# One PSUM bank for the seven first products of a pair, taken in four rounds between the second products

## The chip, the cores and the metric

The kernel runs on one core of one Trainium2 chip. The metric is the device time of one launch in microseconds, the median of several runs. The granted TensorE clock of the profiled execution is 1.000 of full speed.

## The reference

Linear attention in 8 batches of 8 heads, 576 positions of 64 values each, a root-mean-square norm over each head's output, and then a gated feed-forward layer over the 8 x 576 = 4608 rows of 512 values:

```python
kv = np.einsum('bhsd,bhse->bhde', k, v)
out = np.einsum('bhsd,bhde->bhse', q, kv)
rms = np.sqrt(np.mean(out * out, axis=-1, keepdims=True) + 1e-06)
attn = out / rms * g_norm                       # (8, 8, 576, 64)
x = attn.transpose(0, 2, 1, 3).reshape(4608, 512)
h = x @ w_in                                    # 512 -> 2048
g = h * (1.0 / (1.0 + np.exp(-h)))
return g @ w_out                                # 2048 -> 512
```

## The kernel before, in words

The 4608 rows are worked in 9 tiles of 512 (`t` = 0 to 8). The hidden width of 2048 is 16 blocks of 128 (`NF`). Each float32 operand is held as two rounded parts, an upper and a lower, and a product is three matmuls (upper by lower, lower by upper, upper by upper). A matmul here has 256 moving columns.

Tiles 0 and 1 take one block per step. From `t` = 2 on (the third tile) `pair_step` takes two blocks at once, block `i` and block `i + 8`, so a tile is 8 pairs and there are 56 pairs. A pair's two 128 x 512 results come from **seven products** instead of eight, by a scheme of the Strassen kind: sums of weight blocks (`make_sums`, kept in DRAM, loaded back for each pair by `load_sums` into the places `sums0` and `sums1`) meet sums of pieces of x (`sums_of_x`, split into parts by `make_operand`). `product(m, i, out)` issues the six matmuls of product `m` (L662). They are called P1 to P7 in this document, after `m`.

In before, a pair takes two PSUM banks of 512 columns, `bank` (halves `u`, `v`) and `other` (`y`, `z`), and issues all 42 matmuls in the order P1 to u, P2 to v, P6 to y, P7 to z, then P4 to u, P5 to v, P3 to y. ScalarE copies P1 to SBUF (`p1`, L713). VectorE forms the left half of `c1` (L714), `u2` (L715) and `u3` (L716), then `c2` (L726), and the right half of `c1` in two adds (L730, L731). `c1` and `c2` are the pair's two results; `upper_part` runs two Silu on ScalarE for each (L671 to `gh`, L672 in place), and `lower_part` subtracts on VectorE (L675, `gl`).

The **second product** multiplies `gh`, `gl` by blocks of `w_out` and accumulates in four other banks (`acc`, one for 128 rows). `project` is one item by one bank: six matmuls (L493). A pair hands two items to the next pair, so each pair runs eight such groups, 48 matmuls, of the pair before it. `due(n)` issues n groups. In before they stand in one stretch behind the seven products: `due(3)`, `due(3)` and the rest. At a tile's last pair the banks are copied out (L538, `ob`, in turns on VectorE and ScalarE) in the next tile's first pair and stored (L539).

The rest of the attention is spread between these as jobs, by step: `begin` runs the jobs that stand first in a step (copies of `kvm`, L281, and links of the norm's chain), `mid_jobs` and `last_jobs` the others: 80 small kv matmuls (L273) and the query products (L306 to L308) on TensorE, their copies (L312, L313) on ScalarE, the split of q (L293 on ScalarE, L294 on GpSimd), transposes, sums and scaling (L318, L319, L326, L334) on VectorE. `prepare` makes, in a tile's last pair, the next tile's operands: a cast on ScalarE (L653) and a subtraction on VectorE (L654) for each of seven, four after P7 and three after P3. Each engine works through its own queue in the order of the code, and the engines meet by semaphores.

Of the kernel before, what the change touches and what calls it, by code (L numbers as in the profile page):

```python
# [35 lines left out]
def linear_attention_rms_silu_ffn(  # L36
# [22 lines left out]
    nc = tc.nc  # L59
    B, NP, P, S = q.shape  # L60
# [3 lines left out]
    TN = 512  # L64
# [11 lines left out]
    gp = ctx.enter_context(tc.tile_pool(name="gp", bufs=LAG + 1))  # L76
# [28 lines left out]
    for i in range(4):  # L105
        nc.gpsimd.tensor_copy(
            out=both[32 * i:32 * i + 32, 32 * (i ^ 1):32 * (i ^ 1) + 32], in_=ident[32 * i:32 * i + 32, 32 * i:32 * i + 32]
# [106 lines left out]
    def run(*lists):  # L214

        for i in range(max(map(len, lists), default=0)):
            for calls in lists:
                if i < len(calls):
                    calls[i]()
# [255 lines left out]
    def h_bank():  # L475
        return ps_h.tile([P, 512], F32, name="hp", tag="h")
# [51 lines left out]
    def project(t, f, gh, gl, bank, n, cs):  # L528
        first, last = order(t)[0], order(t)[-1]
        w = parts["wo", f]  # L530
        ns = slice(n * P, (n + 1) * P)
        bank = bank[:, :cs.stop - cs.start]
        terms = ((gh, 1), (gh, 0), (gl, 0)) if t else ((gh, 0), (gl, 0), (gh, 1))
        for i, (g, a) in enumerate(terms):
            halves(bank, g[:, ns], w[:, a, cs], f == first and i == 0, f == last and i == 2)
        if f == last:
            ob = tmp.tile([P, S], F32, name="ob", tag="tmp")[:, :cs.stop - cs.start]
            (nc.scalar.copy if n % 2 else nc.vector.tensor_copy)(out=ob, in_=bank)  # L538
            nc.sync.dma_start(out=out[t * TN + n * P:t * TN + (n + 1) * P, cs], in_=ob)  # L539
# [4 lines left out]
    HF, H = NF // 2, TN // 2  # L544
    low, high = slice(0, H), slice(H, TN)
    sums_in_dram = dram.tile([HF, 2, P, 2, 2 * H], F32, name="sums_in_dram")
    operands, x_sums, once = {}, {}, {}
# [43 lines left out]
    def place(name, n, dtype):  # L591

        if name not in once:
            once[name] = block("wi", HF + 2 * n + 1, dtype).rearrange("p a (j n) -> p a j n", n=H)
        return once[name]

    def load_sums(i, *halves):

        for half in halves:
            to = place(f"sums{half}", half, F32R)  # L600
            nc.sync.dma_start(
                out=to.rearrange("p a j n -> p (a j n)").bitcast(F32),
                in_=sums_in_dram[i % HF, half].rearrange("p a n -> p (a n)"),
            )
# [18 lines left out]
    def operand(j):  # L623

        if j < 4:
            return x_second[:, j].rearrange("p a (k n) -> p a k n", k=2)
        if j not in operands:
            operands[j] = spare(j - 4, [P, 2, 2, H], F32R, f"operand{j}")
        return operands[j]
# [20 lines left out]
    def make_operand(m):  # L650
        j, x, _ = seven[m]
        upper, lower = operand(j)[:, 0], operand(j)[:, 1]
        nc.scalar.copy(out=upper, in_=x())  # L653
        nc.vector.tensor_tensor(out=lower, in0=x(), in1=upper.bitcast(F32), op=ALU.subtract)  # L654

    def product(m, i, out):
        j, _, a_of = seven[m]
        x = operand(j)
        n = 0
        for c in range(2):  # L660
            for a, b in ((0, 1), (1, 0), (0, 0)):
                nc.tensor.matmul(  # L662
                    out=out, lhsT=a_of(i, a, c), rhs=x[:, b, c], start=(n == 0), stop=(n == 5)
                )
                n += 1

# [2 lines left out]
    def upper_part(x, gh):  # L669

        nc.scalar.activation(out=gh, in_=x, func=AF.Silu)  # L671
        nc.scalar.activation(out=x, in_=x, func=AF.Silu)  # L672

    def lower_part(x, gh, gl):
        nc.vector.tensor_tensor(out=gl, in0=x, in1=gh.bitcast(F32), op=ALU.subtract)  # L675

    def pair_step(t, i, groups):


        g = t * NF + 2 * i  # L680
        fresh, later = i == HF - 1 and t + 1 < NT, i + 1 < HF or t + 1 < NT

        def due(n):
            while n > 0 and groups:
                n -= (groups[0][-1].stop - groups[0][-1].start) / DM
                project(*groups.pop(0))

        def begin(g):
            run(first_jobs.pop(g, ()))
            run(*[call() for call in chains.pop(g, ())])  # L690

        def prepare(*ms):

            for m in ms if fresh else ():
                make_operand(m)

        begin(g)
        bank, other = h_bank(), h_bank()
        u, v = bank[:, :H], bank[:, H:]
        y, z = other[:, :H], other[:, H:]  # L700
        if "gated" not in once:
            once["gated"] = gp.tile([P, TN], F32, name="gf", bufs=1)
        scratch = place("scratch", 3, F32)
        c1, c2 = [scratch[:, 0].rearrange("p j n -> p (j n)"), once["gated"]][::1 - 2 * (i % 2)]
        p1, u2 = scratch[:, 1, 0], scratch[:, 1, 1]
        u3 = p1
        if g == 2 * NF:
            due(4)
        product(1, i, u)
        product(2, i, v)  # L710
        product(6, i, y)
        product(7, i, z)
        nc.scalar.copy(out=p1, in_=u)  # L713
        nc.vector.tensor_tensor(out=c1[:, low], in0=v, in1=p1, op=ALU.add)  # L714
        nc.vector.tensor_tensor(out=u2, in0=y, in1=p1, op=ALU.add)  # L715
        nc.vector.tensor_tensor(out=u3, in0=z, in1=u2, op=ALU.add)  # L716
        if late_part:
            lower_part(*late_part.pop())
        if later:
            load_sums(i + 1, 0)  # L720
        prepare(1, 2, 6, 7)
        run(mid_jobs.pop(g, ()))
        product(4, i, u)
        product(5, i, v)
        product(3, i, y)
        nc.vector.tensor_tensor(  # L726
            out=c2.rearrange("p (a n) -> p a n", a=2), in0=bank.rearrange("p (a n) -> p a n", a=2),
            in1=u3.unsqueeze(1).to_broadcast([P, 2, H]), op=ALU.add
        )
        nc.vector.tensor_tensor(out=c1[:, high], in0=v, in1=u2, op=ALU.add)  # L730
        nc.vector.tensor_tensor(out=c1[:, high], in0=y, in1=c1[:, high], op=ALU.add)  # L731
        if later:
            load_sums(i + 1, 1)
        prepare(4, 5, 3)
        run(last_jobs.pop(g, ()))
        begin(g + 1)
        hi = [gp.tile([P, TN], F32R, name="gh") for _ in range(2)]
        lo = [gp.tile([P, TN], F32R, name="gl") for _ in range(2)]
        upper_part(c2, hi[0])
        lower_part(c2, hi[0], lo[0])  # L740
        due(3)
        run(mid_jobs.pop(g + 1, ()))
        upper_part(c1, hi[1])
        late_part.append((c1, hi[1], lo[1]))
        due(3)
        run(last_jobs.pop(g + 1, ()))
        due(len(groups))
        return [(t, i + HF, hi[0], lo[0]), (t, i, hi[1], lo[1])]


    first_jobs, mid_jobs, last_jobs, chains = {}, {}, {}, {}
# [86 lines left out]
    with tc.manual_schedule():  # L838
# [5 lines left out]
        for item in ORDER.split():  # L844
            kind, n = item.rstrip("0123456789"), int(item.lstrip("wiopbgq") or 0)
# [20 lines left out]
        p0, p1, p2, p3 = first  # L866
# [134 lines left out]
        for t in range(NT):  # L1001
# [3 lines left out]
            if t >= 2:  # L1005
                for i in range(HF):
                    pend = [(item, sums) for item in pair_step(t, i, [(*item, *old) for item, olds in pend for old in olds])]
                continue
            for step, f in enumerate(order(t)):
                g = t * NF + step  # L1010
# [80 lines left out]
```

## Time and profile before

| | |
|---|---|
| device time, three runs | 817.19, 817.23, 817.42 us; median 817.23 |
| span of the profiled execution | 815.8 us (its device time apart from the span is not recorded) |
| matmul instructions | 7484 |
| DVE instructions, busy | 1036, 533.9 us |
| ACT instructions, busy | 753, 361.6 us |
| POOL instructions, busy | 141, 145.7 us |
| DMA | 122.82 MB, mean 151 GB/s |

The profile is of one execution. PE is TensorE's matmuls and PEld its weight loads, DVE is VectorE, ACT ScalarE, POOL GpSimd and SP the engine that issues the DMAs. Matmuls overlap in the pipeline, so the time between two starts, not the duration of one, tells the rate. A row of the timeline has its start in the span, its time, the engine, the line, the operation, what it writes and reads, its shape and count, and in brackets the idle time before it with what ended that.

### The profile page before, as it was taken

To read this page: it belongs to the slowest core of one execution; us is meant where nothing else is said; L and a number is where in the kernel's file an instruction comes from. 1 tells how busy PE (TensorE), PEld (TensorE's weight loads), DVE (VectorE), ACT (ScalarE), POOL (GpSimd) and SP (SyncE) were. 2 spreads that over 40 slices of the span, in tenths; PEclk is the share of its full clock that TensorE was granted. 3 is DMA by queue.
4 is the path that set the end of the run, shared out by engine and by line. 5 is a ranking of instruction groups with operands and counts; after the bars stand their busy time and mean duration, and the time that the engine had idled before them with its cause. 6 is when DMAs were issued, how large, how long until landed. Compare 5 with 4: busy or idle time off the path is not lost.

```text
span 815.8 us, 18127 instructions
## 1 busy us (share of the span) xinstructions
PE 806.5 (99%) x7484; PEld 801.5 (98%) x7484; DVE 533.9 (65%) x1036; ACT 361.6 (44%) x753; POOL 145.7 (18%) x141
## 2 busy tenths in 40 slices
PE   7999999999999999999999999999999999999998
PEld 7899999999999999999999999999999999999998
DVE  4999956787566677656875767656865663464332
ACT  4887555434552355325532444245532432243222
POOL 2799783322110011000200020001100000000000
DMA  9994012356524444263436451445433343334321
GB/s 345 412 409 126 1 60 90 124 195 228 184 82 162 162 162 156 82 221 118 170 104 211 142 182 64 166 159 174 135 104 104 104 155 105 104 104 155 104 105 53
DMA packets 42277, 122.82 MB, mean 151 GB/s; under 512 B 4690, under 2 KB 4946, under 8 KB 42194
## 3 DMA queue, kind: packets, MB, share of 16 engines
q1 hardware_dynamic: 42194, 121.65, 42.4%
q8 instruction: 59, 0.97, 0.5%
q14 instruction: 24, 0.20, 0.1%
HBM read 103.81 MB, written 17.83 MB: 149 GB/s over the span
## 4 chain that ended last, share of the span: by engine, by line
PE 93%; DMA 4%; POOL 2%; issue 1%; SPq 1%; ACT 0%; POOLq 0%
PE acc L493 46%; PE hp L662 33%; PE hp L493 9%; DMA wo<-in_moe_w_out 3%; PE at L273 2%; PE at L306 1%; PE at L307 1%; PE at L308 1%; DMA early_wo<-in_q 1%; PE at L493 1%; POOL wo L212 1%; SPq L262 1%; POOL wi L212 0%; POOL gl L514 0%; POOL wo_full L178 0%
## 5 line engine op out<-in xcount | busy, mean ns | idle before, releaser
L493 PE MATMUL acc<-wo,gh 128*128 128x256 f32 x2272 | 354.6, 276 | 0.3 <-POOL wo L212 0.3
L493 PEld LDWEIGHTS acc<-wo,gh 128*128 128x128 f32 x2272 | 302.5, 188 | 0.7 <-POOL wo L212 0.5
L493 PE MATMUL acc<-wo,gl 128*128 128x256 f32 x1136 | 222.5, 276 | 0.0
L493 PEld LDWEIGHTS acc<-wo,gl 128*128 128x128 f32 x1136 | 171.7, 188 | 0.0
L662 PE MATMUL hp<-x_second,wi 128*128 128x256 f32 x1344 | 163.1, 276 | 0.0
L662 PEld LDWEIGHTS hp<-x_second,wi 128*128 128x128 f32 x1344 | 157.2, 188 | 0.0
L662 PE MATMUL hp<-operand,wi 128*128 128x256 f32 x1008 | 123.3, 276 | 0.0
L662 PEld LDWEIGHTS hp<-operand,wi 128*128 128x128 f32 x1008 | 118.4, 188 | 0.0
L294 POOL TENSOR_TENSOR ql<-q,qh 128x576 fp32r<-128x576 f32 x24 | 34.8, 1450 | 368.6 <-ACT qh L293 322.8
L713 ACT COPY wi<-hp 128x256 f32<-128x256 f32 x56 | 20.8, 372 | 136.5 <-PE hp L662 136.5
L671 ACT ACTIVATE gh<-gf 128x512 fp32r<-128x512 f32 x56 | 35.4, 632 | 91.9 <-DVE gf L726 80.4
L671 ACT ACTIVATE gh<-wi 128x512 fp32r<-128x512 f32 x56 | 35.5, 634 | 77.4 <-DVE wi L726 65.0
L714 DVE TENSOR_TENSOR gf<-hp,wi 128x256 f32<-128x256 f32 x28 | 11.9, 424 | 81.5 <-ACT wi L713 81.5
L714 DVE TENSOR_TENSOR wi<-hp,wi 128x256 f32<-128x256 f32 x28 | 11.9, 424 | 79.7 <-ACT wi L713 79.7
L493 PE MATMUL hp<-x_second,wi 128*128 128x256 f32 x384 | 46.3, 276 | 0.0
L675 DVE TENSOR_TENSOR gl<-wi,gh 128x512 fp32r<-128x512 f32 x56 | 38.4, 686 | 11.1 <-ACT wi L672 11.1
L493 PE MATMUL hp<-x,wi 128*128 128x256 f32 x360 | 44.5, 278 | 0.8 <-POOL x L444 0.8
L493 PEld LDWEIGHTS hp<-x_second,wi 128*128 128x128 f32 x384 | 44.9, 188 | 0.1
L675 DVE TENSOR_TENSOR gl<-gf,gh 128x512 fp32r<-128x512 f32 x56 | 39.3, 701 | 7.3 <-ACT gf L672 7.3
L493 PEld LDWEIGHTS hp<-x,wi 128*128 128x128 f32 x360 | 42.4, 188 | 1.2 <-POOL x L444 1.0
L715 DVE TENSOR_TENSOR wi<-hp,wi 128x256 f32<-128x256 f32 x56 | 23.8, 426 | 29.6 <-PE hp L662 29.6
L334 DVE SCALAR_TENSOR_TENSOR x<-o,gcol,yT 128x128 f32<-128x128 f32 (+7 forms) x52 | 41.2, 792 | 1.9
(143 smaller groups left out, 995.7 us busy)
## 6 DMA issues: line engine op xcount, KB each, us to landing
wi<-sums_in_dram SPq DMA_DIRECT2D x112, 512.0 KB, 3.4
out<-ob SPq DMA_DIRECT2D x35, 256.0 KB, 2.3
wi<-in_moe_w_in SPq DMA_DIRECT2D x16, 512.0 KB, 7.9
wo<-in_moe_w_out SPq DMA_DIRECT2D x16, 512.0 KB, 8.9
sums_in_dram<-sum_parts SPq DMA_DIRECT2D x16, 512.0 KB, 2.6
k<-in_k SPq DMA_DIRECT2D x28, 288.0 KB, 5.1
v<-in_v SPq DMA_DIRECT2D x28, 288.0 KB, 5.1
q<-in_q SPq DMA_DIRECT2D x28, 288.0 KB, 4.0
```

What stands on the lines that cost most here:

```text
L212: nc.gpsimd.tensor_tensor(out=w[:, 1, :], in0=full, in1=w[:, 0, :].bitcast(F32), op=ALU.subtract)
L262: nc.sync.dma_start(out=t, in_={"k": k, "v": v, "q": q}[name][self.b, self.c])
L273: nc.tensor.matmul(out=self.kv[h], lhsT=self.k[rows, c, :], rhs=self.v[rows, c, :], start=(start and r == 0), stop=(stop and r == 4),)
L294: (nc.vector if self.b == 1 else nc.gpsimd).tensor_tensor(out=self.ql, in0=self.q, in1=self.qh.bitcast(F32), op=ALU.subtract)
L334: nc.vector.scalar_tensor_tensor(out=to, in0=self.o[:, a:e], scalar=gcol, in1=self.yT, op0=ALU.mult, op1=ALU.mult)
L493: nc.tensor.matmul(out=to[:, at:at + 256], lhsT=stationary, rhs=moving[:, at:at + 256], start=start and at == 0, stop=stop and at == n - 256,)
L662: nc.tensor.matmul(out=out, lhsT=a_of(i, a, c), rhs=x[:, b, c], start=(n == 0), stop=(n == 5))
L671: nc.scalar.activation(out=gh, in_=x, func=AF.Silu)
L675: nc.vector.tensor_tensor(out=gl, in0=x, in1=gh.bitcast(F32), op=ALU.subtract)
L713: nc.scalar.copy(out=p1, in_=u)
L714: nc.vector.tensor_tensor(out=c1[:, low], in0=v, in1=p1, op=ALU.add)
L715: nc.vector.tensor_tensor(out=u2, in0=y, in1=p1, op=ALU.add)
```

## The change

The pair uses one bank, the same for all pairs (`once["products"]`), and its seven products come in four rounds, with two groups of second products behind each: P1 to u and P6 to v; P2 added on u and P7 on v; P4 to u anew and P5 to v; P3 added on v. Three products (P2, P7, P3) accumulate on what stands in PSUM. The copy of u and the adds change with that: ScalarE now also copies P1 + P2 to the left half of `c1` (L720), VectorE forms `u2` (L713), `u3` (L721), `c2` (L729) and the right half of `c1` (L740, one add). Jobs of the odd step now begin before P3. The lines of after are one or more higher than those of before from `product` on: the Silu are L672 and L673, the `gl` subtraction L676, and the line of the first products stays L662.

```diff
-    def product(m, i, out):
+    def product(m, i, out, fresh):
...
-                    out=out, lhsT=a_of(i, a, c), rhs=x[:, b, c], start=(n == 0), stop=(n == 5)
+                    out=out, lhsT=a_of(i, a, c), rhs=x[:, b, c], start=fresh and n == 0, stop=n == 5,
+                    skip_group_check=True,
...
-        bank, other = h_bank(), h_bank()
+        if "products" not in once:
+            once["products"] = h_bank()
+            once["gated"] = gp.tile([P, TN], F32, name="gf", bufs=1)
+        bank = once["products"]
         u, v = bank[:, :H], bank[:, H:]
-        y, z = other[:, :H], other[:, H:]
...
         if g == 2 * NF:
             due(4)
-        product(1, i, u)
-        product(2, i, v)
-        product(6, i, y)
-        product(7, i, z)
+        product(1, i, u, True)
+        product(6, i, v, False)
         nc.scalar.copy(out=p1, in_=u)
-        nc.vector.tensor_tensor(out=c1[:, low], in0=v, in1=p1, op=ALU.add)
-        nc.vector.tensor_tensor(out=u2, in0=y, in1=p1, op=ALU.add)
-        nc.vector.tensor_tensor(out=u3, in0=z, in1=u2, op=ALU.add)
+        nc.vector.tensor_tensor(out=u2, in0=v, in1=p1, op=ALU.add)
         if late_part:
             lower_part(*late_part.pop())
+        due(2)
+        run(mid_jobs.pop(g, ()))
+        product(2, i, u, False)
+        product(7, i, v, False)
+        nc.scalar.copy(out=c1[:, low], in_=u)
+        nc.vector.tensor_tensor(out=u3, in0=v, in1=p1, op=ALU.add)
         if later:
             load_sums(i + 1, 0)
         prepare(1, 2, 6, 7)
-        run(mid_jobs.pop(g, ()))
-        product(4, i, u)
-        product(5, i, v)
-        product(3, i, y)
+        due(2)
+        run(last_jobs.pop(g, ()))
+        product(4, i, u, True)
+        product(5, i, v, False)
         nc.vector.tensor_tensor(
             out=c2.rearrange("p (a n) -> p a n", a=2), in0=bank.rearrange("p (a n) -> p a n", a=2),
             in1=u3.unsqueeze(1).to_broadcast([P, 2, H]), op=ALU.add
         )
+        hi = [gp.tile([P, TN], F32R, name="gh") for _ in range(2)]
+        lo = [gp.tile([P, TN], F32R, name="gl") for _ in range(2)]
+        upper_part(c2, hi[0])
+        begin(g + 1)
+        due(2)
+        run(mid_jobs.pop(g + 1, ()))
+        product(3, i, v, False)
         nc.vector.tensor_tensor(out=c1[:, high], in0=v, in1=u2, op=ALU.add)
-        nc.vector.tensor_tensor(out=c1[:, high], in0=y, in1=c1[:, high], op=ALU.add)
+        lower_part(c2, hi[0], lo[0])
         if later:
             load_sums(i + 1, 1)
         prepare(4, 5, 3)
-        run(last_jobs.pop(g, ()))
-        begin(g + 1)
...
-        upper_part(c2, hi[0])
-        lower_part(c2, hi[0], lo[0])
-        due(3)
-        run(mid_jobs.pop(g + 1, ()))
         upper_part(c1, hi[1])
         late_part.append((c1, hi[1], lo[1]))
-        due(3)
         run(last_jobs.pop(g + 1, ()))
         due(len(groups))
```

On TensorE, a plain pair of `t` = 2 (the one of block 6) in before; `operand_2947`, `operand_2951`, `operand_2986` and the first `x_second` are the moving operands of P1, P2, P6 and P7, `wi_1341` carries P4, and the twelve of `wi_2945` are P5 and P3:

```order
L662 MATMUL hp<-operand_2947,wi_664 128x256 x6
L662 MATMUL hp<-operand_2951,wi_664 128x256 x6
L662 MATMUL hp<-operand_2986,wi_2943 128x256 x6
L662 MATMUL hp<-x_second,wi_2943 128x256 x6
L662 MATMUL hp<-x_second,wi_1341 128x256 x6
L662 MATMUL hp<-x_second,wi_2945 128x256 x12
L493 MATMUL acc<-wo_1583,gh 128x256 x4
```

The same pair on TensorE in the change, from the second products behind P1 and P6 to those behind P4 and P5, with the semaphores that each matmul waits for:

```order
L493 MATMUL acc<-wo_1583,gh 128x256 x4
L493 MATMUL acc<-wo_1583,gl 128x256 x2
L662 MATMUL hp<-operand_2951,wi_664 128x256 [waits DVE_49]
L662 MATMUL hp<-operand_2951,wi_664 128x256 x5
L662 MATMUL hp<-x_second,wi_2943 128x256 x6
L493 MATMUL acc<-wo_1583,gh 128x256 x4
L493 MATMUL acc<-wo_1583,gl 128x256 x2
L493 MATMUL acc<-wo_1583,gh 128x256 x4
L493 MATMUL acc<-wo_1583,gl 128x256 x2
L662 MATMUL hp<-x_second,wi_1341 128x256 [waits DVE_49]
L662 MATMUL hp<-x_second,wi_1341 128x256 x5
```

The 42 matmuls that stood together now stand in four pieces with 12 second products behind each, and the first matmul of P2 and of P4 waits for VectorE.

On ScalarE, the join of `t` = 3 and `t` = 4 in before, from the last three casts of `prepare` to the copy of P1 in the next tile's first pair (L713):

```order
L653 CAST x_second<-t_5172 128x512
L653 CAST x_second<-t_5170 128x512
L653 CAST x_second<-x_1_2123 128x512
L281 COPY kvm_90<-at 64x64 x2
L281 COPY kvm_91<-at 64x64 x2
L281 COPY kvm_92<-at 64x64 x2
L281 COPY kvm_93<-at 64x64 x2
L671 ACTIVATE gh<-wi_3138 128x512
L672 ACTIVATE wi_3138<-wi_3138 128x512
L671 ACTIVATE gh<-gf 128x512
L672 ACTIVATE gf<-gf 128x512
L713 COPY wi_3138<-hp 128x256
```

The same place on ScalarE in the change, from the Silu of `c2` to the copy of P1 (now L712):

```order
L672 ACTIVATE gh<-wi_3137 128x512
L673 ACTIVATE wi_3137<-wi_3137 128x512
L281 COPY kvm_90<-at 64x64 x2
L281 COPY kvm_91<-at 64x64 x2
L281 COPY kvm_92<-at 64x64 x2
L281 COPY kvm_93<-at 64x64 x2
L653 CAST x_second<-t_5150 128x512
L653 CAST x_second<-t_5148 128x512
L653 CAST x_second<-x_1_2123 128x512
L672 ACTIVATE gh<-gf 128x512
L673 ACTIVATE gf<-gf 128x512
L712 COPY wi_3137<-hp 128x256
```

The Silu of `c2` moved ahead of the kvm copies and the three casts; the Silu of `c1` and the copy of P1 stand behind them as before.

On TensorE, the first pair of `t` = 2 in the change, from its last second products to the next pair's first (`operand_2947` with `wi_457`):

```order
L493 MATMUL acc<-wo_1162,gh 128x256 x4
L493 MATMUL acc<-wo_1162,gl 128x256 x2
L662 MATMUL hp<-x_second,wi_965 128x256 x6
L662 MATMUL hp<-x_second,wi_2945 128x256 x12
L662 MATMUL hp<-operand_2947,wi_457 128x256 x6
L662 MATMUL hp<-operand_2986,wi_2943 128x256 x6
L493 MATMUL acc<-wo_1251,gh 128x256 x4
```

In before four groups of second products stood between P3 and the next pair's P1; here P4, P5, P3 and the next P1 and P6 follow each other.

More of the change, by code (lines that the diff above doesn't have):

```diff
@@ L697, in pair_step @@
         begin(g)
-        bank, other = h_bank(), h_bank()
+        if "products" not in once:
+            once["products"] = h_bank()
+            once["gated"] = gp.tile([P, TN], F32, name="gf", bufs=1)
+        bank = once["products"]
         u, v = bank[:, :H], bank[:, H:]
-        y, z = other[:, :H], other[:, H:]
-        if "gated" not in once:
-            once["gated"] = gp.tile([P, TN], F32, name="gf", bufs=1)
         scratch = place("scratch", 3, F32)
@@ L734, in pair_step @@
         prepare(4, 5, 3)
-        run(last_jobs.pop(g, ()))
-        begin(g + 1)
-        hi = [gp.tile([P, TN], F32R, name="gh") for _ in range(2)]
-        lo = [gp.tile([P, TN], F32R, name="gl") for _ in range(2)]
-        upper_part(c2, hi[0])
-        lower_part(c2, hi[0], lo[0])
-        due(3)
-        run(mid_jobs.pop(g + 1, ()))
         upper_part(c1, hi[1])
         late_part.append((c1, hi[1], lo[1]))
-        due(3)
         run(last_jobs.pop(g + 1, ()))
```

## The prediction

> **What bounds the kernel now.** I read the page's shares first, then the chain that ended last, then the chain in order of time.
>
> ```profile
> span 815.8 us, 18127 instructions
> PE 806.5 (99%) x7484; PEld 801.5 (98%) x7484; DVE 533.9 (65%) x1036; ACT 361.6 (44%) x753; POOL 145.7 (18%) x141
> PE 93%; DMA 4%; POOL 2%; issue 1%; SPq 1%; ACT 0%; POOLq 0%
> 252.82 4.76 PE hp L662 x42
> 257.58 5.44 PE acc L493 x48
> 263.02 4.76 PE hp L662 x42
> ```
>
> TensorE is both busy and the chain. From t = 2 on a pair is 42 first and 48 second matmuls, 10.20 us: 4.76 / 42 and 5.44 / 48 are both **0.1133 us** a matmul, so neither kind is dearer. I call this a slot. The view of busy time by stage shows how little is left to win:
>
> ```profile
> core 0: us, PE busy (x) PEld busy (x) DVE busy (x) ACT busy (x) POOL busy (x), PEclk, DMA share, GB/s
> 16.00:26.00 10.00, 7.68 (x72) 6.32 (x69) 8.50 (x20) 8.63 (x19) 6.18 (x7) 1.00 1.03 413
> 211.00:816.00 605.00, 601.63 (x5510) 600.38 (x5508) 370.42 (x753) 240.40 (x491) 29.08 (x20) 1.00 0.40 134
> 812.36 0.28 PE L493 MATMUL at<-wo,gl 128*128 128x256 f32 x1
> ```
>
> In the 605 us that the change touches, PE is idle 3.37 us; the last matmul ends at 812.64, 3.13 us before the end of the span (815.77), and the window runs 0.23 past it. Inside the stream nothing is idle. The change keeps every matmul, so it can hardly save PE time; the question is which new wait reaches PE.
>
> **How long a handover takes.** In a plain pair of before:
>
> ```profile
> 273.06 2.20 PE L662 MATMUL hp<-operand,wi 128*128 128x256 f32 x18
> 274.62 0.37 ACT L713 COPY wi<-hp 128x256 f32<-128x256 f32 x1 [3.01 <-PE hp L662]
> 275.02 0.42 DVE L714 TENSOR_TENSOR wi<-hp,wi 128x256 f32<-128x256 f32 x1 [3.03 <-ACT wi L713]
> 276.43 0.42 DVE L716 TENSOR_TENSOR wi<-hp,wi 128x256 f32<-128x256 f32 x1
> 54.86 0.37 ACT L313 COPY o<-at 128x256 f32<-128x256 f32 x1
> 55.28 0.41 PE L306 MATMUL at<-ql,kh 128*128 128x320 f32 x1 [0.74 <-ACT o L313]
> 55.52 0.31 PE L307 MATMUL at<-qh,kl 128*128 128x320 f32 x1
> 55.67 0.31 PE L308 MATMUL at<-qh,kh 128*128 128x320 f32 x1
> ```
>
> P1 and P2 end 12 slots after 273.06, at 274.42; ACT starts at 274.62: **0.20 us** from PE to a reader. It reads u only after P2 too: PE and its readers take a bank whole, in turns. ACT to DVE costs 0.03 (274.99 to 275.02). P4, the 25th matmul, stands at 275.78, and L714 ends at 275.44: before already lives on a margin of 0.34 us there, and of 0.29 at P3 (277.14 against 276.85), and does not stall. The last four rows price a lost margin: ACT ends at 55.23, PE starts at 55.28 (**0.05**), and its next matmul comes 0.24 later where the one after needs 0.15 (**0.09** to restart).
>
> **Plain rounds.** One bank now changes hands four times a pair, each time under two second products (12 slots, 1.36 us), and the first matmul behind waits for VectorE.
>
> ```profile
> L726 DVE TENSOR_TENSOR gf<-hp,wi 128x512 f32<-128x512 f32 x28 | 19.2, 687 | 1.6 <-PE hp L662 0.5
> L731 DVE TENSOR_TENSOR wi<-hp,wi 128x256 f32<-128x256 f32 x28 | 11.9, 425 | 2.9
> L716 DVE TENSOR_TENSOR wi<-hp,wi 128x256 f32<-128x256 f32 x56 | 23.8, 425 | 1.9
> ```
>
> After P1, P6: 0.20 + copy 0.37 + 0.03 + add 0.42 + 0.05 = 1.07; margin 0.29. After P2, P7: the same (the built program lets the add wait for the new ACT copy); 0.29. After P4, P5: 0.20 + 0.69 + 0.05 = 0.94; 0.42. After P3: 0.20 + 0.42 + 0.05 = 0.67; 0.69. So a plain pair costs **0**; its cover is the 12 slots, and if it were gone each handover would cost its 0.67 to 1.07 us plus 0.09. Two VectorE adds of 0.425 us a pair go (L716, L731) and one ACT copy of 0.37 comes; neither engine is full, so these are worth nothing by themselves.
>
> **Joins of tiles: ACT's queue.** ACT and DVE run in order, and the rows of the change show what stands ahead of p1's copy at a tile's end. Before, that copy comes after all 48 second matmuls; now it must be done under 54 slots from P5's end. Durations, from the join after t = 3:
>
> ```profile
> 374.76 1.14 ACT L653 CAST x_second<-t 128x512 fp32r<-128x512 f32 x2
> 375.70 2.70 PE L273 MATMUL at<-v,k 128*64 128x64 f32 x80
> 375.81 0.62 ACT L653 CAST x_second<-x 128x512 fp32r<-128x512 f32 x1
> 378.44 1.74 ACT L281 COPY kvm<-at 64x64 f32<-64x64 f32 x8 [2.02 <-PE at L273]
> 380.20 0.63 ACT L671 ACTIVATE gh<-wi 128x512 fp32r<-128x512 f32 x1
> 380.87 0.63 ACT L672 ACTIVATE wi<-wi 128x512 f32<-128x512 f32 x1
> ```
>
> Count from P5's end. c2 is there at 0.20 + 0.69 = 0.89. ACT: its two Silu 1.30 (380.20 to 381.50) from 0.93 to 2.23; eight kvm copies 1.74, to 3.95 (neighbours overlap by about 0.03 to 0.05); three casts 1.67 (374.76 to 376.43), to 5.6; two Silu of c1 1.30, to 6.85; p1's copy 0.37, to 7.2; then 0.03 + 0.42 + 0.05 to P2: 7.7. PE stands ready after 12 + 6 + 12 + 6 + 6 + 12 = 54 slots, 6.12. The stall is 1.6 us, with 0.09 **1.7**. Four joins have the kvm copies (behind t = 2 to 5, batches 4 to 7): **6.8 us**. Bounds: 1.2 each if the queue overlaps more, 2.5 if casts wait for their inputs.
>
> The last two joins (6 to 7, 7 to 8) lack the kvm copies, and the 2.7 us of kv matmuls that cover the first four casts. From P7's end: the copy is done at 0.57, four casts and their lower parts follow,
>
> ```profile
> L654 DVE TENSOR_TENSOR operand<-x,operand 128x512 fp32r<-128x512 f32 x14 | 9.1, 684 | 0.0
> ```
>
> first cast at 1.15, then four lower parts about 0.64 apart to 3.8, c2 to 4.43, PE at 4.48 against 36 slots, 4.08: 0.40. The next P2: ACT from 4.47 + 1.30 + 1.67 + 1.25 + 0.37, DVE 0.45, 9.5 against 4.48 + 42 slots = 9.24: 0.25. With two restarts 0.83 a join, **1.65** in all; 0 to 3.
>
> **First pair of t = 2.** Its eight second products are spent: four ahead (L706), two and two. Nothing stands between P5 and P3, or between P3 and the next P1. P3 waits 0.94 + 0.09, P1 0.67 + 0.09: **1.8** (1.4 to 2.4).
>
> **x pieces and ob.** In a tile's first pair, DVE has between c2 and the last add an ob copy, a transpose and a scale:
>
> ```profile
> 393.05 0.68 DVE L538 COPY ob<-acc 128x512 f32<-128x512 f32 x1
> 403.12 0.50 DVE L326 STREAM_TRANSPOSE yT<-y 128x320 f32<-128x320 f32 x1
> 403.65 1.79 DVE L334 SCALAR_TENSOR_TENSOR x<-o,gcol,yT 128x320 f32<-128x320 f32 x1
> 410.73 0.55 DVE L334 SCALAR_TENSOR_TENSOR x<-o,gcol,yT 128x320 f32<-128x320 f32 x1
> 403.66 1.44 POOL L294 TENSOR_TENSOR ql<-q,qh 128x576 fp32r<-128x576 f32 x1 [3.53 <-ACT qh L293]
> ```
>
> 0.89 + 0.68 + 0.50 + 0.55 + 0.42 = 3.04 from P5's end, against 30 slots, 3.40: hidden. The same scale took 1.79 where POOL's subtract ran beside it; then the add ends at 4.3 and the stall is 0.9. Pieces are wider in later tiles. I take **0.7** over all tiles; 0 to 4.
>
> **End.** The last two items go bank by bank, so c1's gl is needed at P3's end + 12 + 6 + 4 slots, 2.49. It is there at 0.20 + 0.42 + 1.30 + 0.04 + 0.68 plus about 0.1 of hops, 2.75: 0.3 + 0.09, **0.4** (0 to 0.8).
>
> **Loads.** sums0 is reloaded behind P7 for the next P6: 60 slots, 6.8 us, where it had 78, 8.8; sums1 66, 7.5.
>
> ```profile
> DMA to landing us min/median/max: 3.0/3.4/5.3
> ```
>
> 0.2 + about 0.3 of issue + 5.3 at the worst stays below: 0. Behind a late load would stand all of PE.
>
> **Sum.** 6.8 + 1.65 + 1.8 + 0.7 + 0.4 = 11.35 us. The profiled span of 815.8 becomes 827.1; the median of the runs is 1.43 above that span, so **828.6**. Bounds by term: 4.8 + 0 + 1.4 + 0 + 0 = 6 and 10 + 3 + 2.4 + 4 + 0.8 = 20: 823 to 837.
>
> **Rivals.** (1) *Everything stays hidden.* The join's queue would have to shorten by 1.6 us; for it, the margins of 0.29 that before lives on; against it, no row of the ACT sum is shorter anywhere. Only the stall in t = 2's first pair has no cover at all; 817.2 to 819. (2) *Faster.* VectorE, freed of 112 adds, could let PE run denser. It decides only if a slot shrinks: 1.63 us (0.2%) over 56 x 90 = 5,040 matmuls is 0.32 ns each. Both kinds of matmul have the same slot, and PE idles 0.3 us at most, so I see no such thing; 815.5. (3) *Every round stalls.* If a handover takes over 0.29 us longer than in the rows, the first two rounds of all 56 pairs wait; at 0.4 longer, 112 x (0.11 + 0.09) = 22 us more: 851. Against: L714 and L716 keep their time in every pair. (4) *The clock falls after stalls.* The 13 stalls above, each followed by 24 matmuls at half clock, would cost 13 x 24 x 0.1133 = 35 us: 864. Against: in the window 16 to 26 PE idled 2.3 of 10 us and the granted clock stood at 1.00. The Trainium skill, page "TensorE: Matmul & The Clock Gate", section "A second HAM failure mode: psum-queue depth-cycling", describes this: short idles between groups of matmuls, made by cycling through PSUM, brought the clock gate to oscillate. By that rule the time would be the 864 of this rival; this trace's 1.00 beside 2.3 us of idle speaks against it.
>
> **How the numbers follow.** A change under 0.2% cannot be told from none here. Forecast 0.77; hidden 0.08, most of it within 0.2%; faster 0.02; every round 0.09; clock 0.04. Predicted 828.6. The range, 820 to 838, holds the forecast with its bounds and the upper part of (1); (2), (4) and most of (3) are left out. Faster 0.02, same 0.07, slower 0.91.
>
> **What would show it.** In the profile after: PE with new idle, ended by VectorE, some 11 us in all; the largest at P2 (operand, the second product of a tile's first pair), about 1.6 us, four times, with ACT's queue full ahead of it; two at the start of t = 2; plain pairs still 10.2 us. Wrong: idle in most pairs at P2 or P4 (3), a clock below 1.00 (4), no idle at the joins (1), or waits on the sums' DMA.

## The result and the profile after

| | before | after |
|---|---|---|
| runs on the same chip, us | 817.19 to 817.87, median 817.33 | 833.62, 834.61, 837.46, 841.36; median 836.04 |
| ratio of the times | | 1.0239, 95% interval 1.0204 to 1.0274 |
| span of the profiled execution, us | 815.8 | 839.3 |
| DVE busy, instructions | 533.9 us, 1036 | 480.8 us, 924 |
| ACT busy, instructions | 361.6 us, 753 | 380.1 us, 809 |

The change makes the kernel 2.4% slower, and it makes the time uncertain: the four runs lie 7.7 us apart, those of before 0.7 (817.19 to 817.87; in the later series before ran in 816.56 to 819.16). The profiled execution of after was the longest of the four. The medians of the experiments below are of all runs, while the ratios leave out two runs over 1.5% above the fastest of their program, 830.32 us in experiment 8 and 835.94 us in experiment 9, which no profile explains.

The page of the profile after: the span, the busy times, the chain's shares by engine, the two groups of first products (busy, mean ns of one, and the idle time before them with what ended most of it).

```profile
span 839.3 us, 17964 instructions
...
PE 823.6 (98%) x7484; PEld 817.0 (97%) x7484; DVE 480.8 (57%) x924; ACT 380.1 (45%) x809; POOL 146.9 (18%) x141
...
PE 89%; ACT 3%; DMA 2%; POOL 2%; issue 1%; DVE 1%; SPq 0%; ACTq 0%; POOLq 0%
...
L662 PE MATMUL hp<-x_second,wi 128*128 128x256 f32 x1344 | 184.7, 280 | 0.8 <-DVE gf L729 0.8
...
L662 PE MATMUL hp<-operand,wi 128*128 128x256 f32 x1008 | 136.3, 280 | 6.2 <-DVE wi L713 5.6
```

Two things are to be seen. ACT and DVE, in the chain of before at 0% and not at all, hold 3% and 1% of it, and L662 now idles for VectorE: the waits came. But PE is also **busy** 823.6 us with the same 7484 matmuls that took 806.5. Waits alone can't do that.

The chain in order of time at the join after t = 3 (start, time, what) shows both:

```profile
383.59 0.70 DVE wi L729
...
384.38 0.64 ACT gh L672
...
387.31 1.66 ACT x_second L653 x3
...
390.19 0.38 ACT wi L712
...
390.60 0.44 DVE wi L713
...
391.08 1.68 PE hp L662 x12
392.76 1.41 PE acc L493 x12
394.18 1.41 PE hp L662 x12
```

P5 ended 0.20 ahead of the first row, at 383.39. The copy of P1 is done at 390.57, 7.18 later (predicted 7.2), and P2 starts at 391.08, 7.69 later (predicted 7.7). Behind it, twelve matmuls take **1.41** us. In a plain pair of t = 2, in the same execution, they take 1.36:

```profile
269.67 1.36 PE hp L662 x12
271.03 1.36 PE acc L493 x12
```

The slot has gone from 0.1133 us to 0.1178, by 3.9%, for first and second products alike. The view of busy time by stage shows that the granted clock (the column behind POOL) did not change, and that PE has no idle to speak of there:

```profile
core 0: us, PE busy (x) PEld busy (x) DVE busy (x) ACT busy (x) POOL busy (x), PEclk, DMA share, GB/s
...
391.00:474.00 83.00, 82.92 (x758) 82.72 (x758) 46.04 (x98) 33.87 (x73) 6.09 (x4) 1.00 0.43 141
...
748.00:832.00 84.00, 84.00 (x713) 83.80 (x712) 26.99 (x51) 26.78 (x49) 0.00 (x0) 1.00 0.31 101
```

The **long slot**, as I call it (the expectations below call it the slow cadence), fills most of t = 4 to 8 and nothing of t = 3. It can be seen to end and to begin in the chain of the last join:

```profile
742.02 1.41 PE acc L493 x12
743.43 0.84 PE hp L662 x6
744.28 1.36 PE acc L493 x12
745.64 1.36 PE hp L662 x12
747.00 1.36 PE acc L493 x12
748.36 1.49 PE hp L662 x12
749.85 1.41 PE acc L493 x12
```

A row of PE work behind other PE work starts here at the end of the matmul before, 0.12 to 0.16 us behind its own first start. At P3 of a tile's last pair (the row of 743.43) and at P2 of the next (748.36) PE lost some 0.1 us in a break. Behind the first the slot is short again, behind the second long.

From the starts of all matmuls of the trace, against before: breaks in the stream of 256-column matmuls add 9.3 us, longer slots 14.8 us (some 3,300 matmuls by 4.45 ns), and PE came to its first L662 0.66 us earlier. Together that is 23.5, the difference of the spans.

### The profile page after: what moved, and what is told of

Read it like the earlier page. It is cut to its first block, busy times and chain, and to the rows that moved or that the text cites. A ratio compares the mean times of both kernels' runs of the same rounds, so it can differ in the third digit from the quotient of the medians.

```text
span 839.3 us, 17964 instructions
## 1 busy us (share of the span) xinstructions
PE 823.6 (98%) x7484; PEld 817.0 (97%) x7484; DVE 480.8 (57%) x924; ACT 380.1 (45%) x809; POOL 146.9 (18%) x141
## 4 chain that ended last, share of the span: by engine, by line
PE 89%; ACT 3%; DMA 2%; POOL 2%; issue 1%; DVE 1%; SPq 0%; ACTq 0%; POOLq 0%
PE acc L493 44%; PE hp L662 32%; PE hp L493 8%; PE at L273 2%; DMA wi<-in_moe_w_in 1%; PE at L306 1%; PE at L307 1%; PE at L308 1%; POOL wo L212 1%; ACT x_second L653 1%; DMA early_wi<-in_q 1%; DMA k<-in_k 1%; ACT kvm L281 1%; PE at L493 1%; ACT gh L672 1%
## 5 line engine op out<-in xcount | busy, mean ns | idle before, releaser
L493 PE MATMUL acc<-wo,gh 128*128 128x256 f32 x2272 | 359.4, 279 | 0.2 <-POOL wo L212 0.2
L493 PEld LDWEIGHTS acc<-wo,gh 128*128 128x128 f32 x2272 | 306.7, 189 | 0.4 <-POOL wo L212 0.4
L493 PE MATMUL acc<-wo,gl 128*128 128x256 f32 x1136 | 225.5, 279 | 0.0
L662 PE MATMUL hp<-x_second,wi 128*128 128x256 f32 x1344 | 184.7, 280 | 0.8 <-DVE gf L729 0.8
L662 PEld LDWEIGHTS hp<-x_second,wi 128*128 128x128 f32 x1344 | 168.9, 189 | 1.4 <-DVE gf L729 1.0
L662 PE MATMUL hp<-operand,wi 128*128 128x256 f32 x1008 | 136.3, 280 | 6.2 <-DVE wi L713 5.6
L662 PEld LDWEIGHTS hp<-operand,wi 128*128 128x128 f32 x1008 | 125.2, 189 | 7.2 <-DVE wi L713 6.4
L294 POOL TENSOR_TENSOR ql<-q,qh 128x576 fp32r<-128x576 f32 x24 | 36.0, 1500 | 383.8 <-ACT qh L293 362.5
L672 ACT ACTIVATE gh<-wi 128x512 fp32r<-128x512 f32 x56 | 35.4, 632 | 89.5 <-DVE wi L729 79.9
L672 ACT ACTIVATE gh<-gf 128x512 fp32r<-128x512 f32 x56 | 35.4, 633 | 86.4 <-DVE gf L729 78.3
L721 DVE TENSOR_TENSOR wi<-hp,wi 128x256 f32<-128x256 f32 x56 | 23.8, 425 | 77.3 <-ACT gf L720 40.8
L713 DVE TENSOR_TENSOR wi<-hp,wi 128x256 f32<-128x256 f32 x56 | 23.7, 424 | 69.0 <-ACT wi L712 68.8
L493 PE MATMUL hp<-x_second,wi 128*128 128x256 f32 x384 | 46.3, 277 | 0.0
L493 PEld LDWEIGHTS hp<-x_second,wi 128*128 128x128 f32 x384 | 44.9, 188 | 0.1
L729 DVE TENSOR_TENSOR gf<-hp,wi 128x512 f32<-128x512 f32 x28 | 19.4, 692 | 44.0 <-PE hp L662 44.0
L712 ACT COPY wi<-hp 128x256 f32<-128x256 f32 x56 | 20.8, 372 | 44.1 <-PE hp L662 44.0
L729 DVE TENSOR_TENSOR wi<-hp,wi 128x512 f32<-128x512 f32 x28 | 19.4, 692 | 35.4 <-PE hp L662 34.8
L676 DVE TENSOR_TENSOR gl<-gf,gh 128x512 fp32r<-128x512 f32 x56 | 38.2, 682 | 0.8 <-ACT gf L673 0.8
L676 DVE TENSOR_TENSOR gl<-wi,gh 128x512 fp32r<-128x512 f32 x56 | 38.2, 682 | 0.0
```

Source lines behind the costliest of these rows:

```text
L294: (nc.vector if self.b == 1 else nc.gpsimd).tensor_tensor(out=self.ql, in0=self.q, in1=self.qh.bitcast(F32), op=ALU.subtract)
L493: nc.tensor.matmul(out=to[:, at:at + 256], lhsT=stationary, rhs=moving[:, at:at + 256], start=start and at == 0, stop=stop and at == n - 256,)
L662: nc.tensor.matmul(out=out, lhsT=a_of(i, a, c), rhs=x[:, b, c], start=fresh and n == 0, stop=n == 5, skip_group_check=True,)
L713: nc.vector.tensor_tensor(out=u2, in0=v, in1=p1, op=ALU.add)
L721: nc.vector.tensor_tensor(out=u3, in0=v, in1=p1, op=ALU.add)
L729: nc.vector.tensor_tensor(out=c2.rearrange("p (a n) -> p a n", a=2), in0=bank.rearrange("p (a n) -> p a n", a=2), in1=u3.unsqueeze(1).to_b ...
```

## The experiments

The theory after the result: the new waits cost what they are long, and besides a restart can leave PE in the long slot, which stays until another break. Rivals: the long slot belongs to the new use of PSUM (one bank, accumulation, four rounds); or it is a clock; or it needs idle of some length. Each series of runs has runs of before on the same chip beside it, and long slots came on all four chips of the experiments. Where an expectation names e2, e3, e4 and e5, these are experiments 2, 3, 6 and 4 here.

**1. Three casts later.** Products 4, 5 and 3 of the next tile's operands are cast in that tile's first pair, behind P6, not ahead of c1's Silu.

```diff
+        while held:
+            make_operand(held.pop(0))
         due(2)
...
-        prepare(4, 5, 3)
+        held.extend((4, 5, 3) if fresh else ())
```

> The change, with the three casts behind P3 of a tile's last pair moved into the next tile's first pair, behind u2. Both theories: the four waits of 1.57 us at P2 behind t = 2 to 5 go (ACT's queue is 1.7 us shorter there), 6 to 7 us of idle less; the waits of the first pair of t = 2 (1.3 us) stay, and a few of about 0.1 us. Lock (a wait of PE can leave it at 117.8 ns a matmul until a later break): the long stretches at 117.8 start less often, only behind the small waits that are left; 820 to 832. Pattern (the 117.8 ns belong to the four rounds on one bank, whatever PE waits): about 15 us of slow matmuls stay, 829 to 831.

Measured: median 830.04 (829.02 to 833.44), ratio 1.0167 (1.0142 to 1.0192). The four waits of 1.6 us are gone: breaks over before fell from 9.3 to 2.9 us, longer slots from 14.8 to 8.8. Three long stretches stayed. The chain shows one begin 2.8 us behind a short break (a wait of 0.02 us at P2, at 476.31, and 0.1 to restart), with short slots between:

```profile
476.45 1.50 PE hp L662 x12
477.95 1.36 PE acc L493 x12
479.31 1.42 PE hp L662 x12
480.73 1.41 PE acc L493 x12
```

In the starts, the last short slots are followed at 479.15 by one of 120 ns, and then by 117.8 on average. So the long waits were costed rightly, and the long slot needs no long wait.

**2. All waits out.** Also the other waits are moved away: the casts of 1, 2, 6 and 7 and the held ones spread over the rounds, no `due(4)` at the start of t = 2, the jobs of the odd step behind P3, the split of q later, the end in another order.

```diff
-        if g == 2 * NF:
-            due(4)
...
+        prepare(1)
...
-        prepare(1, 2, 6, 7)
+        prepare(2, 6, 7)
...
-        run(mid_jobs.pop(g + 1, ()))
         product(3, i, v, False)
...
+        run(mid_jobs.pop(g + 1, ()))
```

> The change with every wait taken out that I can count: casts spread over two pairs, no four groups ahead of t = 2's first pair, jobs of the odd step behind the add after P3, the split of q a third of a step later, the last two items one after the other. The four rounds on one bank, the accumulating products and all 42 + 48 matmuls of a pair are as in the change. Lock: no wait, no stretch at 117.8 ns, 817 to 819. Pattern: the idle goes (8 us), the slow matmuls stay, 826 to 832. If only the idle of the joins matters: 817 to 819 as well, but then e3 shows no slow matmuls.

Measured: median 819.9 (819.13 to 822.84), ratio 1.0040 (1.0026 to 1.0053). In its profiled execution (821.1 us) PE is busy 807.0 us, before 806.5, and no long stretch stands in it:

```profile
PE 807.0 (98%) x7484; PEld 801.6 (98%) x7484; DVE 483.9 (59%) x924; ACT 380.6 (46%) x809; POOL 145.5 (18%) x141
```

So the seven products in four rounds of one bank run at the old pace where nothing disturbs them, and the rival of PSUM falls. What was left over 817 to 819: its end order (6.23 us behind the last matmul's start, before 3.41) and one wait of 0.47 at P2 in t = 6. No profile shows the two longest runs, 822.22 and 822.84.

**3. Waits in the kernel before.** One matmul into the `at` bank and three VectorE copies of it onto u, ahead of P1 in the first pair of t = 3 to 8, so that P1 waits.

```diff
+        if i == 0 and t > 2:
+            stop_at, x = at_bank(), operand(4)[:, 0, 0]
+            nc.tensor.matmul(out=stop_at[:, :H], lhsT=x[:, :P], rhs=x, start=True, stop=True)
+            for _ in range(3):
+                nc.vector.tensor_copy(out=u, in_=stop_at[:, :H])
         product(1, i, u)
```

> The kernel before with one wait put in ahead of the first product of t = 3 to 8, six in all: one more matmul into a spare bank, then three VectorE copies from it onto u, for which P1 waits; each costs about 1.5 us of idle, 0.1 of restart and 0.1 for the matmul, 10 us in all: 827 to 828. Lock: behind some of the six the matmuls take 117.8 ns until the next kv block, 828 to 846, and the times spread by some us from run to run. Pattern: 113.3 ns throughout, 827 to 828 and no spread.

Measured: median 839.45 (835.5 to 842.51), ratio 1.0266 (1.0227 to 1.0306). Six breaks of 1.9 us each make 829; the rest is long slots, in the profiled execution 298.4 to 383.8 and 570.0 to 660.1, that is behind two of the six; behind the other four the slot is short. So the long slot does not belong to the changed kernel: before falls into it too.

**4. One wait.** The same in t = 7 alone (`t == 7`).

> The kernel before with one wait only, ahead of the first product of t = 7, behind which no kv block comes any more. Idle of the wait 1.7 us, its matmul 0.1, restart 0.1: 819.2 if only the wait costs. Lock: runs of two kinds, 819.2 where PE comes back at 113.3 ns and about 825.6 where it stays at 117.8 to the end (1440 matmuls of 4.45 ns are 6.4 us). If the waits do not lock PE singly: 819.2 in every run.

Measured: median 826.0, all four runs 825.58 to 826.47, ratio 1.0104 (1.0091 to 1.0117). The timeline of PE at that place, after which no kv block comes any more:

```profile
644.16 0.28 PE L711 MATMUL at<-operand 128*128 128x256 f32 x1
646.05 2.36 PE L662 MATMUL hp<-operand,wi 128*128 128x256 f32 x18 [1.61 <-DVE hp L713]
648.25 2.99 PE L662 MATMUL hp<-x_second,wi 128*128 128x256 f32 x24
651.08 0.63 PE L493 MATMUL acc<-wo,gh 128*128 128x256 f32 x4
```

A wait that is worth 1.9 us cost 8.7: the 24 matmuls of the second row of L662 take 2.83 us to the next row's start, where before takes 2.72 (645.87 to 648.59), and so it goes to the end of the kernel.

**5. A shorter wait.** One VectorE copy in place of three.

> Before, with one wait at the start of tile 7 as in the run with one wait, but made of one VectorE copy instead of three: about 0.7 us instead of 1.6 us. If the slow cadence comes on any restart, the time is the wait and the same slow stretch up to the end: 825, in all runs. If it needs a long wait, it is the wait alone: 818.2. If it depends on the moment of the restart, runs of both kinds, 818 and 825.

Measured: median 821.54, but eight runs of one program in **two groups**: 817.71, 818.05, 818.54, 818.61 and 824.46, 825.13, 825.45, 825.91. The wait is 0.59 us. The groups lie 7.0 us apart; the 1,480 matmuls left at that place, by 4.45 ns, are 6.6. The profiled execution is one of the second group, long from the wait to the end; that the first group had short slots is read from its times. So a restart may end in either slot, and the same program does both.

**6. Small matmuls in the changed kernel.** Most long stretches end behind the 80 small kv matmuls or behind a wait. So eight matmuls of 64 columns into the `at` bank, results unused, stand behind P7 of the first pair of t = 3 to 8; in a second kernel one.

```diff
+        if i == 0 and t > 2:
+            small_at = at_bank()
+            for _ in range(8):
+                nc.tensor.matmul(out=small_at[:D, :D], lhsT=kvm[0][:, :D], rhs=kvm[0][:, :D], start=True, stop=True)
```

> The change, with eight float32 matmuls of 64 columns (into a spare bank, results unused) behind P7 of a tile's first pair, t = 3 to 8, so behind the wait at P2. They cost about 0.55 us each time, 3.3 us. Lock, with a reset by such matmuls as the kv blocks seem to do: the slow stretches that start at P2 end 1.4 us later, 825 to 832. Lock without a reset by them, or pattern: 836 to 842.

> e4 with one small matmul instead of eight. Cost about 0.6 us each time instead of 1.2, so 3.5 us less than e4 if one of them ends a slow stretch as well as eight: 831 to 834. If one does not end it: 836 to 845, with slow stretches up to the kv blocks as in the change.

Measured: with eight, median 836.31 (835.04 to 838.4), ratio 1.0233 (1.0216 to 1.025); with one, 833.83 (830.44 to 836.02), ratio 1.0208 (1.019 to 1.0227). With eight, longer slots fell from 14.8 to 3.3 us over before, and three long stretches end right behind them:

```profile
394.17 0.87 PE L662 MATMUL hp<-x_second,wi 128*128 128x256 f32 x6
394.97 1.15 PE L723 MATMUL at<-kvm 128*64 128x64 f32 x16
396.05 0.74 PE L493 MATMUL acc<-wo,gh 128*128 128x256 f32 x4
396.62 0.39 PE L493 MATMUL acc<-wo,gl 128*128 128x256 f32 x2
396.86 0.62 PE L493 MATMUL acc<-wo,gh 128*128 128x256 f32 x4
397.31 0.39 PE L493 MATMUL acc<-wo,gl 128*128 128x256 f32 x2
```

(The trace counts two for each of these small matmuls: sixteen for the eight, and 80 for the 40 that the code issues in a kv block.) Four matmuls of 396.86 take 0.45 us to the next row, 0.113 each; the six of P7 ahead of the block have the longer time of 0.87 in place of 0.84. But the block takes 1.08 us where 0.55 was expected, and with a break of 0.1 on either side six of them cost 7.7 us: so the median, which alone would speak for no reset, is that of after. A fourth stretch, 661.3 to 742.5, ran on over them. With one, the profiled execution (830.44) has long slots only in the last 4 us of its matmuls, and the first products behind all its waits at P2 were short before the small matmul came: it can't tell whether one ends a stretch. No profile shows what made the other three, 832.32 to 836.02, longer.

**7. Small matmuls behind the one wait.** The same eight behind P7 in t = 7, in before with its one long wait.

> e5 with eight float32 matmuls of 64 columns behind P7 of the same pair, 2.7 us behind the wait (about 1.2 us by e4). If these end a slow stretch as the kv blocks seem to: 820.3 to 820.8 in every run or nearly every one. If they do nothing: 820.4 and 826.8, as in e5.

Measured: eight runs, five at 819.94 to 821.01 and three at 826.99 to 827.14 (median 820.94, ratio 1.0068, 1.0041 to 1.0094). Without them it was 826 four times in four. The profiled execution is one of the three long ones, and its stretch ran on over the small matmuls. That they ended a stretch in the other five is not shown: these may have come back short from the wait itself, as four of six did in experiment 3. What the traces show is three stretches ended by such a block in experiment 6 and two that ran on, one there and one here.

**8. All waits out, the end mended.** As experiment 2, the last groups first item first on two banks, then bank by bank.

> e2 with the order of the very last groups mended: two banks of the first item ahead, then both items bank by bank, so that copies and stores out are spread again (e2's tail behind the last matmul is 6.23 us against 3.41 before). Lock: 817.0 to 817.8, the time of before, since PE is then as full as before. If the rounds on one bank cost something of their own: 819 or more.

Measured: median 820.45, ratio 1.0029 (1.0016 to 1.0042), and again a spread: four runs at 817.56 to 817.89, as before, seven at 819.67 to 822.37, and one at 830.32. By the median the second answer would hold; the four runs speak against it, since a cost of the rounds would stand in every run. The chain of the profiled one, of 822.37, has a long stretch from 298.8 to 382.1:

```profile
296.04 1.36 PE hp L662 x12
297.40 1.36 PE acc L493 x12
298.76 1.53 PE hp L662 x12
300.30 1.41 PE acc L493 x12
```

P2 was kept there 0.02 us by the add behind P1's copy (a slot of 0.130 ahead of it), and PE restarted into the long slot. That stretch is worth 3.0 us. Another 1.8 lie at the end, which is not mended in this execution: from the start of the last matmul to the end of the span it takes 5.18 us, before 3.41.

**9. The kvm copies shared.** In experiment 8's kernel half of the eight kvm copies go to VectorE, to bring the copy of P1 forward.

```diff
+                if h and self.b > 1:
+                    nc.vector.tensor_copy(out=self.kvm[d, d], in_=self.kv[h])
+                else:
+                    nc.scalar.copy(out=self.kvm[d, d], in_=self.kv[h])
```

> The order without the long waits and with the mended end, and four of the eight kvm copies at each join given to VectorE, so that ScalarE comes some 0.8 us earlier to the Silu of c1 and to the copy of P1 in the next tile's first pair, the place of the wait of about 0.1 us behind which the profile of the order before had its slow stretch. Theory (a wait, however short, lets TensorE fall into 117.8 ns a matmul): without that wait all runs stand together at 817.3 to 818.5, and the profile has 113.3 ns throughout. Rival (the new order of the products itself falls into the slow cadence at times, or another wait of this kernel does it): runs still spread from 817.6 to 822.

Measured: median 823.71 (five runs at 822.02 to 824.01, one at 835.94), ratio 1.0072 (1.0059 to 1.0085): neither answer, for the edit made a wait of its own. VectorE at the join:

```profile
295.67 0.23 DVE L282 COPY kvm<-at 64x64 f32<-64x64 f32 x1 [0.27 <-ACT kvm L284]
296.17 0.23 DVE L282 COPY kvm<-at 64x64 f32<-64x64 f32 x1 [0.27 <-ACT kvm L284]
296.43 0.42 DVE L745 TENSOR_TENSOR gf<-hp,wi 128x256 f32<-128x256 f32 x1
```

The two engines took turns, 0.25 us each, and the last add of c1 (L745), which P1 of the next tile waits for, stood behind them. In this execution PE waited 1.1 us at P1 in four tiles, and restarted into the short slot all four times; it has no long stretch at all.

**10. The waits filled.** If it takes idle to lose the short slot, PE should be kept at work: 84 matmuls of 256 columns into an unused PSUM bank, results unused, as many at each place as the wait is long.

```diff
+        def fill(n):
+            x = operand(1)[:, 0, 0]
+            for _ in range(n):
+                nc.tensor.matmul(out=once["spare"][:, :H], lhsT=x[:, :P], rhs=x, start=True, stop=True)
...
+        fill(7 * (t == 2 and i == 1))
         product(1, i, u, True)
...
+        if i == 0:
+            fill({2: 0, 7: 2, 8: 2}.get(t, 15))
         product(2, i, u, False)
...
+        fill(9 * (t == 2 and i == 0) + 2 * (i == HF - 1 and t in (6, 7)))
         product(3, i, v, False)
```

> The change with its waits filled: 84 matmuls of 256 columns into an unused half of a PSUM bank, results not used, put ahead of the matmuls that waited, as many as the wait is long by the trace (9 and 7 at the start of tile 2, 15 ahead of P2 at four joins, 2 and 2 at each of the last two joins). Their 84 slots, 9.5 us, take the place of about 9 us of waits. Theory (the cadence of 117.8 ns is entered when TensorE restarts after being idle): no idle, no slow cadence; 817.3 + 9.5 + 0.3 = 827, all runs close together. Rival (the waits for other engines, or the order of the products, bring the slow cadence by themselves, idle or not): 834 to 842 as in the change.

Measured: median **848.45** (848.27 to 849.26), ratio 1.0384 (1.0369 to 1.04). Worse than either: no wait is left at these places, and the four runs lie within 1 us of each other, with the long slot nearly everywhere in the profiled one.

```profile
302.00 1.36 PE acc L493 x12
303.36 1.79 PE hp L701 x15
305.15 1.41 PE hp L662 x12
306.57 1.41 PE acc L493 x12
```

The fifteen fillers take 0.120 us each, a slot that no row of matmuls of the kernel has, and behind them stands 1.41 for twelve, without any idle. The long slot fills all from 217.6 but for the 7 us between each kv block and the next fillers and the last 4 us: some 4,750 matmuls of the kernel, 20.9 us. With the 84 fillers, 10.0 us, that is 848.1, and the small breaks and the earlier start cancel.

**11. The short wait filled, in before.** Experiment 5 with eight such matmuls behind the one that the copy waits for.

```diff
+            for _ in range(8):
+                nc.tensor.matmul(out=y, lhsT=x[:, :P], rhs=x, start=True, stop=True)
```

> Before with the short wait of one VectorE copy at the start of tile 7, and eight matmuls of 256 columns (results not used) behind the matmul that the copy waits for, so that TensorE works until the copy is done. Nine slots, 1.02 us. Theory (idle, then the slow cadence): 818.3 in all runs. Rival (the wait itself): runs in two groups again, about 818 and 825.

Measured: median 825.23, four runs 824.94 to 825.53, ratio 1.0098 (1.0081 to 1.0115). Not two groups but one, the long one:

```profile
644.03 0.12 PE at L711
644.14 0.96 PE hp L715 x8
645.10 4.95 PE hp L662 x42
650.05 5.65 PE acc L493 x48
```

PE has no idle at this place, and 42 and 48 matmuls take 4.95 and 5.65 us, before 4.76 and 5.44. That idle is needed is refuted, and two groups, as my rival had it, did not come in these four runs. The nine take 0.120 each from the first on. They read their weights and their moving columns from one place, which no other matmul there does; whether that makes their slot was not tried. It also puts a limit on experiments 3, 4, 5 and 7: each has one such matmul ahead of its wait, so they don't tell which of the two did it. After, experiment 1 and experiment 8 have none, and fall into the long slot behind their waits alone.

No version ran faster than before. The nearest by its ratio, experiment 8, reaches 817.6 in its best runs.

## Why the prediction was right in kind, and what it missed

The direction, and the waits, came as forecast; the predicted 828.6 was 7.4 us short of the median, for a cause that is no term of the sum. That 836 still lies in the range of 820 to 838 is luck: the room above the forecast was meant for the x pieces (up to 4) and the last joins (up to 3), which came to 0.1 and 0.46, and the long slot filled it. The longest run, 841.36, lies above the range.

- **Four joins**, predicted 1.7 each: PE stood 1.57 us (1.68 between two starts), and 0.11 more to restart: 1.68 each, 6.7 of the 6.8. The queue's working (7.2 to the copy, 7.7 to P2) held to 0.02.
- **Last two joins**, predicted 0.83 each: 0.2 each, a wait of 0.04 at P3 and two restarts of 0.1; 1.65 was too much by 1.2. At the join of t = 7 and 8, `c2` was done 4.23 us behind P7's end (743.26, counted 4.43), PE's 36 slots were long there and took 4.24 (counted 4.08), and ACT needed 4.31 from the Silu of `c2` to the end of P1's copy (743.35 to 747.66, counted 4.59).
- **First pair of t = 2**, predicted 1.8: the two waits are 0.95 and 0.68 by their starts, and with two restarts of 0.11 it is 1.85.

```profile
218.51 0.96 PE L662 MATMUL hp<-x_second,wi 128*128 128x256 f32 x6 [0.78 <-DVE gf L729]
220.00 1.65 PE L662 MATMUL hp<-operand,wi 128*128 128x256 f32 x12 [0.52 <-DVE wi L740]
```

- **x pieces and ob**, 0.7: one break of 0.1, at P1 of the second pair of t = 7. **End**, 0.4: 0.26. **Loads**, 0: no wait on the sums.
- **Plain rounds**, 0: right as far as waits go; the margins hold, and the pairs of t = 2 take 10.20 us as before (264.23 to 274.43 in the chain).
- Sum of the waits with their restarts: 9.3 measured, 11.35 predicted. The terms that were too large hid part of the one that was missing.
- **The step that failed** is none of the edits but the ground under them: that both kinds of matmul "have the same slot", 0.1133, and that a lost margin costs its length and 0.09 to restart. Both were read from a kernel whose stream is broken by nothing but kv blocks once tile 2 runs, and whose trace shows no other slot. The missing term is the slot after a break, 14.8 us in the profiled execution. If the shorter runs had the same waits, which no profile shows, it was less there: 833.62 less the 817.33 of before and 8.6 (9.3 less the earlier start) leaves 7.7, and 841.36 leaves 15.4.

Of the rivals, *all hidden*, *faster* and *every round stalls* are out: waits stand at the joins, at the start of t = 2 and at the end. *The clock falls after stalls* came nearest, since it looked for the cost behind the stall and not in it; but it priced it at half the clock for 24 matmuls, and what came is 3.9% for 613 to 708 at a stretch, with the granted clock at 1.00. The oscillation of the clock gate that the Trainium skill describes (page "TensorE: Matmul & The Clock Gate", section "A second HAM failure mode: psum-queue depth-cycling") did not show here: the two stages above have 1.00 beside the long slot, and experiment 2 cycles one bank four times a pair at the short one.

## What to carry to other kernels

Where TensorE's stream is the bound and has no breaks, a new wait can cost far more than its length (in the profiled execution of after 9.3 us of breaks and 14.8 us of longer slots): look at the time of twelve matmuls behind it, not only at the idle ahead of it. Dummy matmuls in the gap are no safe remedy, since those tried here, with a slot of their own, set the pace of the thousand behind them; what helped was to move the wait away, as in experiment 2. And where one program's runs fall into groups, profile one of each before averaging them.

## What the runs showed that I had not expected

- A stream of weight loads and 256-column matmuls ran at two steady slots, 113.3 and 117.8 ns, with a granted clock of 1.00 in both. The Trainium skill, page "TensorE: Matmul & The Clock Gate", section "Back-to-back issue gap", has the spacing of such a stream set by weight load and matmul together, and gives one figure for a shape (128 and 512 columns); here one shape had two. The 4.45 ns stand between a weight load and its own matmul: before, a load starts 110.0 ns ahead of its matmul, in the long stretches 114.4, while the next load starts 3.3 ns behind the matmul in both.
- The long slot began behind waits of 0.02 to 1.6 us, and behind matmuls at 120 ns with no wait. In the profiled executions it ended behind every kv block that it met, behind a block of eight small matmuls three times in five, behind all eight waits that fell into it (the shortest of 0.04 us), or not before the end of the kernel. The same program did both (experiment 5). What PE holds on to in it, and why one restart takes it and another does not, stays open.
- The 80 small kv matmuls take 2.63 us in the chain whether the stream ahead has the short slot or the long one:

```profile
470.14 1.41 PE acc L493 x12
471.55 2.63 PE at L273 x80
```

In t = 2, with 1.36 for twelve ahead of them, they take 2.63 as well (from 290.07). The query products of 320 columns keep their time too: in after, L307 takes 146.6 ns to the next start in the short stretches (8 of them) and 146.8 in the long (12), where 3.9% more would be 152. L307 of 256 columns goes from 113.4 to 117.4. So the long slot is not a slower clock of the engine.
